# A recurrence and a max-of-two layer on one core: wd made two chunks of units at a time by strided columns, and lower_bound read by ScalarE's queue

## The chip, the cores and the metric

One NeuronCore of a Trainium2 chip, and a program of one launch. The metric is the device time of a run in microseconds (us). The kernel before took 380.85 us (median of 3 runs, 380.81 to 381.16). A ratio below is the mean time of one kernel's fast runs over that of the other's fast runs of the same rounds, so not quite the ratio of the medians that stand beside it. TensorE does the products and the transposes, VectorE, ScalarE and GpSimd the work on elements, and the sync, ScalarE and GpSimd queues issue the loads. L436 is line 436 of the kernel; in the changed kernel the lines quoted below stand five further down (L436 is L441 there). A chain of waits is read back from the last instruction: at each step to what released it, or to the instruction before it on its engine.

## The reference, cut to what matters

```python
sig = 1.0 / (1.0 + np.exp(-f_logit))                 # x, f_logit: 4 x 6144 x 256
f = lower_bound + (1.0 - lower_bound) * sig          # lower_bound: 256
h = f[:, t] * h + (1.0 - f[:, t]) * x[:, t]          # for each t; y[:, t] = h
g = np.maximum(y @ w1, y @ w2)                       # w1, w2: 256 x 1024
out = g @ w_out                                      # w_out: 1024 x 256
```

The kernel uses 1 − f = (1 − lower_bound)·(1 − sig): with om = 1 − lower_bound folded into the weights, it needs max(y w1, y w2) = y w1 + relu(y (w2 − w1)). So `wd` = om·(w2 − w1) feeds the first layer, and the part y·w1·w_out goes through `w13`, made from `w1T` and `wob` (w_out in half precision).

Of the kernel before, what the change touches and what calls it, by code (L numbers as in the profile page):

```python
# [12 lines left out]
AF = mybir.ActivationFunctionType  # L13
ENG = mybir.EngineType
P = 128
# [3 lines left out]
def kernel(  # L19
# [10 lines left out]
    nc = tc.nc  # L30
# [14 lines left out]
    for b in range(B):  # L45
        t = 0
# [49 lines left out]
    def fetch(c, s):  # L96
        b, t0, nt, _ = chunks[c]
        src = srcs[s][b, t0 : t0 + nt, :]
        if by_xbar(c, s):
            nc.gpsimd.dma_start(  # L100
                out=pieces(scratch[s][c % NSCR][:]), in_=pieces(src)
            )
        else:
            nat = inpool.tile([P, TB // P, D], HALF, name=("fT", "xT")[s])
            nc.gpsimd.dma_start(  # L105
                out=nat[:].rearrange("p i d -> p (i d)"),
                in_=src.rearrange("(p i) d -> p (i d)", p=P),
            )
            held[c, s] = nat
# [3 lines left out]
    def fetch_first(k):  # L113
        nt = TB // 2
        for s in range(2):
            raw = opool.tile([P, nt // P, D], FP32, name="osb")
            nc.sync.dma_start(  # L117
                out=raw[:],
                in_=srcs[s][0, k * nt : (k + 1) * nt, :].rearrange(
                    "(p i) d -> p i d", p=P  # L120
                ),
            )
            raws[k, s] = raw
# [37 lines left out]
    def turn_steps(j):  # L161
        b, t0, nb, c, o = blocks[j]
        steps = []
        for s in range(2):
            dst = ps_o.tile([P, KC, TB], HALF, name="ps")
            ns = nb // P
            turned[j, s] = dst[:].rearrange("p k (i m) -> p k m i", i=ns)
            for q in range(ns):
                for h in range(KC):
                    steps.append(  # L170
                        (
                            dst[:, h, q * P : (q + 1) * P],
                            held[c, s][:, q, h * P : (h + 1) * P],
                        )
                    )
        return steps
# [14 lines left out]
    def y_of(j, k):  # L191
        return rts[j, k][:, KH, :]
# [123 lines left out]
    ident_f = const.tile([P, P], FP32)  # L316
    make_identity(nc, ident_f[:])
    ident = const.tile([P, P], HALF)
    om = const.tile([P, KC], FP32)
    nom = const.tile([P, KC], FP32)  # L320
    lbc = const.tile([P, KC], FP32)
    seen = const.tile([1, 16], HALF)
    waited = const.tile([P, 1], FP32)
    warm = const.tile([P, 1], FP32)
    wob = wpool.tile([P, FC, D], HALF)
    wd = wpool.tile([P, KC, DFF], HALF)
# [6 lines left out]
    NQ = FC // NG  # L333
    w2n = [rpool.tile([P, KC, NQ * P], FP32, name="r") for g in range(NG)]
    w1n = [rpool.tile([P, KC, NQ * P], FP32, name="r") for g in range(NG)]
    w1s = [rpool.tile([P, KC, NQ * P], FP32, name="r") for g in range(NG)]
# [13 lines left out]
    def scale_w1(g):  # L350
        for kc in range(KC):
            nc.scalar.mul(w1s[g][:, kc, :], w1n[g][:, kc, :], om[:, kc : kc + 1])

    def half_w1(g, copy):
        for kc in range(KC):
            copy(out=w1h[g][:, kc, :], in_=w1s[g][:, kc, :])

    def make_wd(g):
        for kc in range(KC):
            nc.vector.scalar_tensor_tensor(  # L360
                out=wd[:, kc, g * NQ * P : (g + 1) * NQ * P],
                in0=w2n[g][:, kc, :],
                scalar=om[:, kc : kc + 1],
                in1=w1s[g][:, kc, :],
                op0=ALU.mult,
                op1=ALU.subtract,
            )

    def unit_cols(fc):

        g, q = divmod(fc, NQ)
        return slice(g * NQ * P + q, (g + 1) * NQ * P, NQ)

    def turn_w1(g):
        pt = ps_o.tile([P, NQ, KC, P], HALF, name="ps")
        for q in range(NQ):
            for kc in range(KC):
                nc.tensor.transpose(
                    pt[:, q, kc, :], w1h[g][:, kc, q : NQ * P : NQ], ident[:]
                )  # L380
        return pt

    def keep_w1T(g, pt):
        nc.vector.tensor_copy(
            out=w1T[:, g * NQ : (g + 1) * NQ, :],
            in_=pt[:].rearrange("p q k d -> p q (k d)"),
        )
# [42 lines left out]
    def first_layer(j, fc):  # L430
        k, g = divmod(fc, KH)
        if fc % 2 == 0:
            dts["d"] = ps_d.tile([P, 2, TB], FP32, name="dT")
        dT = dts["d"]
        for kc in range(KC):
            nc.tensor.matmul(  # L436
                dT[:, fc % 2, :],
                lhsT=wd[:, kc, unit_cols(fc)],
                rhs=y_of(j, kc),
                start=(kc == 0),  # L440
                stop=(kc == KC - 1),  # L441
            )
        if fc % 2:
            nc.scalar.activation(  # L444
                out=rts[j, k][:, g - 1 : g + 1, :].rearrange(
                    "p q (i m) -> p q i m", m=P
                ),
                in_=dT[:].rearrange("p q (m i) -> p q i m", m=P),
                func=AF.Relu,
            )  # L450
# [166 lines left out]
        return [runner(s) for s in steps]  # L617

    with tc.manual_schedule():
        nc.sync.dma_start(out=lbc[:], in_=lower_bound.rearrange("(h p) -> p h", p=P))  # L620
        nc.vector.tensor_copy(out=ident[:], in_=ident_f[:])
        nc.vector.tensor_scalar(
            out=om[:], in0=lbc[:], scalar1=-1.0, scalar2=1.0, op0=ALU.mult, op1=ALU.add
        )
        nc.vector.tensor_scalar_add(out=nom[:], in0=lbc[:], scalar1=-1.0)
        fetch_first(0)
        fetch_first(1)
        for g in range(NG):
# [3 lines left out]
            out=wob[:].rearrange("p (g q) c -> p g (q c)", g=NG),  # L632
            in_=moe_w_out.rearrange("(g p q) c -> p g (q c)", g=NG, q=NQ),
        )
        for c in range(1, 6):
            for s in range(2):
                fetch(c, s)
        nc.scalar.activation(out=warm[:], in_=om[:, 0:1], func=AF.Sigmoid)
        wt = ps_d.tile([P, 2, 2 * TB], HALF, name="dT")
        for q in range(8):  # L640
            nc.tensor.transpose(wt[:, 0, 0:P], ident[:], ident[:])
# [9 lines left out]
            nc.tensor.transpose(wt[:, 0, 0:P], ident[:], ident[:])  # L651
        scale_w1(0)
        half_w1(0, nc.scalar.copy)
        make_wd(0)
        pt = turn_w1(0)
        keep_w1T(0, pt)
        scale_w1(1)
        for fc in range(4):
            first_layer(0, fc)
        half_w1(1, nc.vector.tensor_copy)  # L660
        make_wd(1)
        pt = turn_w1(1)
        for fc in range(4, 8):
            first_layer(0, fc)
        keep_w1T(1, pt)
        steps = turn_steps(1)
        make_w13(0)
        turn(steps[:8])
# [118 lines left out]
```

## The kernel before: what the change touches

The work is done in blocks of 512 tokens. Block 0 has a prologue of its own, in two halves, while the weights arrive. The order of statements is the order on each engine. Cuts are marked with `# ...`.

```python
def make_wd(g):                              # one of two groups of 512 units
    for kc in range(KC):
        nc.vector.scalar_tensor_tensor(
            out=wd[:, kc, g * NQ * P : (g + 1) * NQ * P],
            in0=w2n[g][:, kc, :], scalar=om[:, kc : kc + 1], in1=w1s[g][:, kc, :],
            op0=ALU.mult, op1=ALU.subtract)

def unit_cols(fc):                           # unit chunk fc: every fourth column of its group
    g, q = divmod(fc, NQ)
    return slice(g * NQ * P + q, (g + 1) * NQ * P, NQ)
# ...
nc.sync.dma_start(out=lbc[:], in_=lower_bound.rearrange("(h p) -> p h", p=P))
nc.vector.tensor_copy(out=ident[:], in_=ident_f[:])
# om = 1 - lbc, nom = lbc - 1, both on VectorE
fetch_first(0); fetch_first(1)               # f and x of block 0, sync queue
for g in range(NG):
    fetch_w(g)                               # w1, w2 in two groups, sync queue
pool_waits(w1n[0][:, 0, 0:1])                # GpSimd waits for the first weight piece,
# ... then issues wob and f, x of blocks 1 to 3, then the scratch loads
nc.scalar.activation(out=warm[:], in_=om[:, 0:1], func=AF.Sigmoid)
# ... 8 dummy transposes
first_bf16(0, 0, nc.vector.tensor_copy)      # casts of f and x, first half of block 0
first_bf16(0, 1, nc.vector.tensor_copy)
first_turn(0)                                # transposes
first_recurrence(0)                          # sigmoid, decay, drive, scans
first_bf16(1, 0, nc.scalar.copy); first_bf16(1, 1, nc.scalar.copy)
first_turn(1); first_recurrence(1)
for q in range(24):                          # dummy transposes that keep TensorE busy
    nc.tensor.transpose(wt[:, 0, 0:P], ident[:], ident[:])
scale_w1(0)
half_w1(0, nc.scalar.copy)
make_wd(0)
pt = turn_w1(0)
keep_w1T(0, pt)                              # copy of the transposed w1, VectorE
scale_w1(1)
for fc in range(4):
    first_layer(0, fc)
half_w1(1, nc.vector.tensor_copy)            # casts, VectorE
make_wd(1)
pt = turn_w1(1)
for fc in range(4, 8):
    first_layer(0, fc)
keep_w1T(1, pt)
# ... make_w13 (needs w1T and wob), then block 1: transposes of f and x, and so on
```

## Time and profile before

| | us |
|---|---|
| median of the timed runs | 380.85 |
| the profiled execution itself | 381.55 |
| its span in the profile | 379.8 |

The lines of this profile are in the prediction below.

### The profile page before, as it was taken

Reading aid. Unit: us, or ns where it says so; the run is one execution under the profiler, and the core shown is the slowest. Engines: PE = TensorE matmul, PEld = TensorE weight load, DVE = VectorE, ACT = ScalarE, POOL = GpSimd, SP = SyncE. Lnnn points to the kernel's source line nnn. Section 1 sums busy time; section 2 is a strip of 40 time slices with the busy share of each in tenths; the row PEclk is TensorE's granted clock in tenths of the full one; section 3 lists DMA queues with packets and bytes.
Section 4 is the critical chain, followed back from the end, with each engine's and each line's share of the span. In section 5 each row is a group of like instructions: output and inputs, shape, how many; then the busy total and the mean of one; then the engine's idle time right before and its main releaser. Section 6 shows DMA issues by size and latency. Waiting matters only on the chain.

```text
span 379.8 us, 9454 instructions
## 1 busy us (share of the span) xinstructions
PE 369.1 (97%) x4076; PEld 279.9 (74%) x4076; DVE 333.0 (88%) x402; ACT 300.3 (79%) x406; POOL 37.5 (10%) x79
## 2 busy tenths in 40 slices
PE   4999999999999999999999999999999999999995
PEld 3677766777777777777777777777777777777784
DVE  4696789999999999999999999999999999999721
ACT  4846788798798888888888887987888888888740
POOL 1500103101201101102011011011011021000000
PEclk9999999999999999999999999999999999999999
DMA  7994999989999999999899999999999999970223
GB/s 249 242 226 98 265 162 256 167 156 289 195 195 276 180 190 251 202 172 285 143 257 190 219 251 278 127 263 223 182 263 212 188 268 211 192 265 3 110 113 113
DMA packets 103389, 77.17 MB, mean 203 GB/s; under 512 B 93554, under 2 KB 94066, under 8 KB 102642
## 3 DMA queue, kind: packets, MB, share of 16 engines
q1 hardware_dynamic: 100514, 51.13, 59.8%
q0 software_dynamic: 2544, 25.17, 34.5%
q8 instruction: 32, 0.52, 0.6%
q10 hardware_dynamic: 288, 0.26, 0.2%
q14 instruction: 11, 0.09, 0.1%
HBM read 53.48 MB, written 48.23 MB: 268 GB/s over the span
## 4 chain that ended last, share of the span: by engine, by line
PE 89%; DMA 4%; DVE 3%; POOL 1%; SPq 1%; ACT 0%; issue 0%
PE ps L605 42%; PE dT L436 41%; PE ps L482 6%; DMA xT<-in_x_dram 3%; DMA r<-in_moe_w_dram 1%; DVE r L230 1%; DVE S L506 1%; SPq L117 0%; PE ps L180 0%; DVE osb L496 0%; DVE v L223 0%; POOL fT L105 0%; DVE ff L213 0%; ACT r L444 0%; POOL wob L631 0%
## 5 line engine op out<-in xcount | busy, mean ns | idle before, releaser
L444 ACT ACTIVATE r<-dT 128x1024 f16<-128x1024 f32 x192 | 195.8, 1022 | 53.2 <-PE dT L436 53.0
L436 PE MATMUL dT<-r,wd 128*128 128x512 f16 x768 | 225.4, 379 | 1.0 <-DVE wd L360 0.5
L605 PEld LDWEIGHTS <-S 128*128 128x128 f16 x1680 | 110.9, 101 | 37.6 <-issue 0.6
L605 PEld LDWEIGHTS <-r 128*128 128x128 f16 x1260 | 87.3, 101 | 36.6
L230 DVE TENSOR_TENSOR_SCAN r<-ff,r,v 128x512 f16<-128x512 f16 x88 | 108.2, 1270 | 0.8
L605 PE MATMUL ps<-t,S 128*128 128x128 f16 x1260 | 97.8, 219 | 0.0
L436 PEld LDWEIGHTS <-wd 128*128 128x128 f16 x768 | 67.6, 113 | 6.4 <-DVE wd L360 1.1
L506 DVE TENSOR_TENSOR S<-r 128x2560 f16<-128x2560 f16 x42 | 62.4, 1485 | 10.1 <-ACT r L444 10.0
L605 PE MATMUL ps<-wob,r 128*128 128x128 f16 x672 | 67.4, 219 | 0.0
L506 DVE TENSOR_TENSOR S<-r,S 128x2560 f16<-128x2560 f16 x42 | 61.9, 1474 | 0.0
L285 ACT ACTIVATE u<-fT 128x512 f16<-128x512 f16 x88 | 56.0, 636 | 1.0 <-DMA fT<-scr 1.0
L213 DVE TENSOR_SCALAR ff<-u,nom 128x512 f16<-128x512 f16 (+1 forms) x98 | 31.3, 346 | 9.7 <-ACT u L207 5.3
L348 POOL CAST waited<-fT 128x1 f32<-128x1 f16 x21 | 10.8, 513 | 279.5 <-DMA fT<-scr 279.5
L605 PE MATMUL ps<-w,r 128*128 128x128 f16 x168 | 36.8, 219 | 0.0
L562 DVE TENSOR_TENSOR osb<-ps,sn 128x512 f32<-128x512 f32 x42 | 28.7, 684 | 6.8 <-ACT osb L560 5.3
L605 PE MATMUL ps<-t,r 128*128 128x128 f16 x420 | 33.4, 219 | 0.0
L605 PE MATMUL ps<-wob,S 128*128 128x128 f16 x336 | 31.4, 219 | 0.0
L223 DVE TENSOR_TENSOR v<-u,xT 128x1024 f16<-128x1024 f16 x44 | 30.1, 684 | 0.2 <-DMA xT<-scr 0.2
L482 PEld LDWEIGHTS <-r 128*128 128x128 f16 x240 | 23.9, 101 | 6.9
L482 PE MATMUL ps<-wob,r 128*128 128x256 f16 x192 | 26.8, 273 | 0.0
L550 ACT COPY sn<-ps 128x512 f32<-128x512 f32 x42 | 24.6, 587 | 1.1 <-PE ps L605 0.9
L560 ACT COPY osb<-ps 128x512 f32<-128x512 f32 x42 | 24.4, 582 | 0.5 <-PE ps L605 0.5
(56 smaller groups left out, 134.8 us busy)
## 6 DMA issues: line engine op xcount, KB each, us to landing
out_dram<-osb SPq DMA_DIRECT2D x47, 512.0 KB, 3.9
scr<-in_f_logit_dram POOLq DMA_DIRECT2D x22, 512.0 KB, 7.4
scr<-in_x_dram POOLq DMA_DIRECT2D x22, 512.0 KB, 10.4
r<-in_moe_w_dram SPq DMA_DIRECT2D x4, 512.0 KB, 6.8
fT<-in_f_logit_dram POOLq DMA_DIRECT2D x3, 256.0 KB, 9.2
xT<-in_x_dram POOLq DMA_DIRECT2D x3, 256.0 KB, 11.1
osb<-in_f_logit_dram SPq DMA_DIRECT2D x2, 256.0 KB, 4.5
osb<-in_x_dram SPq DMA_DIRECT2D x2, 256.0 KB, 4.1
```

The costliest lines, as they stand in the source:

```text
L213: nc.vector.tensor_scalar(out=ff[:, h, cols], in0=u[:, h, cols], scalar1=nom[:, h : h + 1], scalar2=1.0, op0=ALU.mult, op1=ALU.add,)
L223: nc.vector.tensor_tensor(out=like(v[:, :, cols], xT), in0=like(u[:, :, cols], xT), in1=xT, op=ALU.mult,)
L230: nc.vector.tensor_tensor_scan(out=y_of(j, h), data0=ff[:, h, o : o + TB], data1=v[:, h, o : o + TB], initial=0.0 if t0 == 0 else y_of(j - ...
L285: nc.scalar.activation(out=mids[p + NBLK, "u"][:, h, cols], in_=held[c, 0][:, h, cols], func=AF.Sigmoid, scale=-1.0,)
L436: nc.tensor.matmul(dT[:, fc % 2, :], lhsT=wd[:, kc, unit_cols(fc)], rhs=y_of(j, kc), start=(kc == 0), stop=(kc == KC - 1),)
L444: nc.scalar.activation(out=rts[j, k][:, g - 1 : g + 1, :].rearrange("p q (i m) -> p q i m", m=P), in_=dT[:].rearrange("p q (m i) -> p q i ...
L482: nc.tensor.matmul(ps[:, r, :], lhsT=left, rhs=right, start=(s == 0 and (r == 0 or j == NBLK - 1)), stop=(s == n - 1 and (r == 1 or j == N ...
L506: nc.vector.tensor_tensor(out=t[:], in0=a, in1=b, op=op)
L550: nc.scalar.copy(out=t[:], in_=bank[b][:])
L560: nc.scalar.copy(out=dst, in_=bank[b][:])
L562: nc.vector.tensor_tensor(out=dst, in0=bank[b][:], in1=snap[name][:], op=ALU.add)
L605: nc.tensor.matmul(bank[b][:, i, :], lhsT=a[:, k, cols], rhs=w, start=fresh, stop=after is not None, skip_group_check=True,)
```

## The change

Its intent is to let the first layer of block 0 begin after a quarter of wd instead of a half, to take the copies of w1T out from between, and to give the head of the sync queue to the first loads of f and x. Unit chunk fc uses every fourth column of its group, so two chunks are two neighbouring columns out of each four.

```diff
--- before.py
+++ after.py
@@ -355,13 +355,18 @@
         for kc in range(KC):
             copy(out=w1h[g][:, kc, :], in_=w1s[g][:, kc, :])
 
-    def make_wd(g):
+    def make_wd(g, pair):
+
+
+        def cut(t):
+            return t.rearrange("p (n q) -> p n q", q=NQ)[:, :, 2 * pair : 2 * pair + 2]
+
         for kc in range(KC):
             nc.vector.scalar_tensor_tensor(
-                out=wd[:, kc, g * NQ * P : (g + 1) * NQ * P],
-                in0=w2n[g][:, kc, :],
+                out=cut(wd[:, kc, g * NQ * P : (g + 1) * NQ * P]),
+                in0=cut(w2n[g][:, kc, :]),
                 scalar=om[:, kc : kc + 1],
-                in1=w1s[g][:, kc, :],
+                in1=cut(w1s[g][:, kc, :]),
                 op0=ALU.mult,
                 op1=ALU.subtract,
             )
@@ -617,12 +622,13 @@
         return [runner(s) for s in steps]
 
     with tc.manual_schedule():
-        nc.sync.dma_start(out=lbc[:], in_=lower_bound.rearrange("(h p) -> p h", p=P))
+        nc.scalar.dma_start(out=lbc[:], in_=lower_bound.rearrange("(h p) -> p h", p=P))
         nc.vector.tensor_copy(out=ident[:], in_=ident_f[:])
+        nc.scalar.activation(out=warm[:], in_=ident_f[:, 0:1], func=AF.Sigmoid)
+        nc.vector.tensor_scalar_add(out=nom[:], in0=lbc[:], scalar1=-1.0)
         nc.vector.tensor_scalar(
             out=om[:], in0=lbc[:], scalar1=-1.0, scalar2=1.0, op0=ALU.mult, op1=ALU.add
         )
-        nc.vector.tensor_scalar_add(out=nom[:], in0=lbc[:], scalar1=-1.0)
         fetch_first(0)
         fetch_first(1)
         for g in range(NG):
@@ -635,7 +641,6 @@
         for c in range(1, 6):
             for s in range(2):
                 fetch(c, s)
-        nc.scalar.activation(out=warm[:], in_=om[:, 0:1], func=AF.Sigmoid)
         wt = ps_d.tile([P, 2, 2 * TB], HALF, name="dT")
         for q in range(8):
             nc.tensor.transpose(wt[:, 0, 0:P], ident[:], ident[:])
@@ -651,18 +656,20 @@
             nc.tensor.transpose(wt[:, 0, 0:P], ident[:], ident[:])
         scale_w1(0)
         half_w1(0, nc.scalar.copy)
-        make_wd(0)
-        pt = turn_w1(0)
-        keep_w1T(0, pt)
         scale_w1(1)
-        for fc in range(4):
-            first_layer(0, fc)
+        pt0 = turn_w1(0)
+        for pair in range(2):
+            make_wd(0, pair)
+            for fc in range(2 * pair, 2 * pair + 2):
+                first_layer(0, fc)
         half_w1(1, nc.vector.tensor_copy)
-        make_wd(1)
-        pt = turn_w1(1)
-        for fc in range(4, 8):
-            first_layer(0, fc)
-        keep_w1T(1, pt)
+        pt1 = turn_w1(1)
+        for pair in range(2):
+            make_wd(1, pair)
+            for fc in range(4 + 2 * pair, 6 + 2 * pair):
+                first_layer(0, fc)
+        keep_w1T(0, pt0)
+        keep_w1T(1, pt1)
         steps = turn_steps(1)
         make_w13(0)
         turn(steps[:8])
```

## The prediction

> **What bounds the kernel now.** I read the page first, its busy shares and its forty slices.
>
> ```profile
> PE 369.1 (97%) x4076; PEld 279.9 (74%) x4076; DVE 333.0 (88%) x402; ACT 300.3 (79%) x406; POOL 37.5 (10%) x79
> ...
> PE   4999999999999999999999999999999999999995
> ```
>
> TensorE is busy in every slice but the first and the last. The next question is whether it ever waits once it is full, so I took the busy time of each engine by stretch.
>
> ```profile
> 2.00:22.50 20.50, 16.19 (x139) 12.10 (x136) 13.71 (x27) 12.47 (x21) 6.74 (x12) 1.00 1.11 278
> 22.50:30.00 7.50, 7.23 (x61) 5.19 (x62) 6.97 (x14) 4.99 (x6) 0.00 (x0) 1.00 1.00 214
> 30.00:367.00 337.00, 336.70 (x3802) 254.64 (x3800) 309.91 (x357) 280.38 (x379) 30.06 (x61) 1.00 0.97 201
> ```
>
> The columns are stretch, length, busy PE, PEld, DVE, ACT, POOL, then granted clock, DMA share, GB/s. From 30 to 367 us TensorE lacks 0.30 us in 337. No instruction of the change runs in there, so the change can only move the moment at which this block of work begins. Everything it edits lies before 20 us. The prologue is therefore what counts, and I read the chain of waits for its first 26 us.
>
> ```profile
> 0.74 0.44 SPq L620
> 1.18 0.06 issue
> 1.25 0.45 SPq L117
> ...
> 3.16 5.50 DMA r<-in_moe_w_dram
> 8.66 0.05 issue
> 8.72 0.28 POOL waited L348
> 8.99 0.81 POOL wob L631
> ...
> 11.39 11.08 DMA xT<-in_x_dram
> 22.48 0.05 issue
> 22.52 0.62 PE ps L180 x8
> 23.14 2.18 PE ps L482 x20
> ```
>
> The columns are start, length, what. The chain begins with the sync queue issuing lower_bound (L620), then x and f of block 0 and the weights. GpSimd waits for the first weight piece before it issues its own loads, and the x tile of block 2 lands at 22.48 us. That landing releases TensorE's transposes (L180). Neither the wd instructions (L360) nor the first layer (L436) of block 0 are on it. Is the DMA time in the chain latency or throughput? The DMA share of 1.11 in the first stretch above (overlapping records take it over 1) says throughput: from about 2.5 us on the transfers are limited by the engines, not by waiting.
>
> The timeline of TensorE shows how close the other path comes:
>
> ```profile
> 15.13 1.70 PE L436 MATMUL dT<-r,wd 128*128 128x512 f16 x7 [0.23 <-DVE wd L360]
> 16.67 1.04 PE L392 MATMUL ps<-wob,w1T 128*128 128x256 f16 x8
> 17.55 0.62 PE L180 MATMUL ps<-ident,fT 128*128 128x128 f16 x8
> ...
> 21.61 0.61 PE L180 MATMUL ps<-ident,fT 128*128 128x128 f16 x8
> 22.52 0.62 PE L180 MATMUL ps<-ident,xT 128*128 128x128 f16 x8 [0.30 <-DMA xT<-in_x_dram]
> ```
>
> Between the end of block 0's first layer and the landing TensorE runs without a gap, then waits only 0.30 us for x of block 2. So the compute path has 0.30 us of slack against the transfer path.
>
> **What the Trainium skill says.** "Trainium Kernel Development and Optimization", Key Constraints: transfers issued from the sync, scalar and GpSimd queues share 16 DMA engines, and several issuers save only the sequencer's issue time. The trace gives that issue time: 0.44 us for lower_bound, with the next issue at 1.25 instead of 0.74.
>
> "SBUF — State Buffer", Door 1: SBUF has 16-byte lines and wants at least two hits in a line. A pair of fp32 columns out of every four is two hits in 16 bytes, so the strided cut should not slow the reads. The kernel before has no such VectorE read, so its trace can't say.
>
> "VectorE: DVE Perf Modes", The TRN2 errata: instructions that read SBUF carry a fixed extra cost, so halving one doesn't halve its time. The trace agrees: a scan of 256 columns took 0.678 us, one of 512 took 1.272 us.
>
> "TensorE: Matmul & The Clock Gate", What's actually happening: the array starts at half rate and its start-to-start is 106.7 ns cold and 55.6 ns warm for 128 columns. The trace agrees: 24 dummy weight loads (L651) take 2.60 us, 108 ns each, and later 8 transposes go by in 0.45 us.
>
> **The change, part by part.**
>
> *lower_bound off the sync queue.* It removes one issue from the head of that queue: 1.25 − 0.74 = 0.51 us. The four loads of block 0 and the four weight pieces are issued 0.51 us earlier. Fine slices of the DMA share show about 0.2 from 1.8 to 2.3 us at 2 GB/s, which I take for the small pieces of lower_bound; the big load starts after them. The capacity regained is about 0.5 us × 0.8 = 0.4 us, with little loss as lower_bound now interleaves. As the engines are then full until the landing at 22.48, that landing moves by 0.4 to 0.5 us; I take 0.45. lower_bound itself may land a little later, since ScalarE issues it at about 0.73 and loads its table (1.28 us) after; its first use, in the decay at 5.76, has nearly 3 us of room. The warm-up activation no longer waits for om, so the table is ready by about 2.5, before the sigmoid at 5.13.
>
> *wd in pairs.* One instruction over 512 columns takes 0.744 us and the next starts about 0.65 later. At one element per 0.96 GHz cycle, 256 columns fewer save 0.27 us: an estimate of 0.48 us long, 0.38 apart. Eight of them occupy about 3.0 us instead of 2.6, so VectorE does 0.4 us more. What is won: w1T's copy leaves the way between the wd groups (0.60 us), and the second group's half-casts, wd and products move forward. On before's clock: the first pair is ready at 11.95, when the transposes of w1 free TensorE anyway; the second at 12.71; products 0 to 3 are issued by 13.64 rather than 14.05. Casts end at 13.37, the second group's transposes run to about 14.1, its pairs are ready at 14.1 and 14.9, and the last product is issued at 15.65 rather than 16.65. That is 1.0 us on TensorE.
>
> But what comes next needs other things. The product of w1T and wob (L392) needs both copies of w1T, now last on VectorE: 14.8 + 2 × 0.65 = 16.1. It needs wob as well, issued at 8.94 and 7.3 us to landing, 16.24. Then come f of block 1 (9.80 + 7.7 = 17.5) and x of block 2 at 22.48. So of the 1.0 us some 0.4 survive to the start of L392 and nothing survives the wait for x: the wait of 0.30 merely grows to about 0.7. Its worth at the end is 0.0 to 0.05 us.
>
> *Sum.* Removed from the path: 0.45 + 0.0. Added to it: nothing. 380.85 − 0.45 = 380.40 us. One later point could catch this gain: the first layer of block 4 begins at 45.61, and the second scan that it reads ends at 45.70 for a product due at 45.83, so a slack of about 0.1. That scan hangs on the scratch transfers and crossbar transposes, which come from the same GpSimd queue and the same full DMA engines, so I expect it to move along.
>
> **Rivals.**
>
> *A. The pairs pay in full.* TensorE's first layer of block 0 ends 1.0 us sooner and carries through, with 0.45 of the queue: 379.4. For it: TensorE does wait for wd (0.26 and 0.23). Against it: the chain passes through the landing at 22.48, and wob's landing at 16.24 stops it sooner.
>
> *B. Nothing moves.* The small packets of lower_bound now compete with the first big load, or the landing at 45.7 keeps its place: 380.8. For it: full DMA engines, and 0.1 us of slack there. Against it: the idle engines before 2.3 us.
>
> *C. The strided cut is slow.* Should each column cost double, eight instructions take 0.27 more each, 2.1 us; the copies of w1T end near 18.2 and L392 starts 1.1 to 1.5 us after its old place, of which 0.3 is slack: about 381.5 with the queue's gain. Against it are the line rule above and the small pieces.
>
> *D. TensorE warms later.* The clock rises near 12 us now. If it rose one product group later, 16 products would take 0.2 us more each, partly hidden: up to +2 us. The dummy transposes stay and move with the loads, so I give it little.
>
> **Range and chances.** Even A and D together stay within 0.6% of the time, while 2% is 7.6 us. The only way to over 2% is a different state of the chip or an interplay in the full region that the trace doesn't hint at. The three runs before spread over 0.35 us. I give 379.8 to 380.9 at 8 in 10: A lies below it, B inside it, C and D above it. Chances: faster 0.01, same 0.98, slower 0.01.
>
> **What would show it.** In the changed profile: the first sync issue is x or f at about 0.74; the first cast starts near 3.55 instead of 4.00; the weight landing that releases GpSimd is near 8.2; eight wd instructions of about 0.48 us; the wait of L180 for x of block 2 grows to 0.5 to 0.8 us and ends near 22.0; the stretch from 30 to 367 is as full as before. I am wrong if that wait vanishes (then compute was the bound), if x lands at 22.5 as before (the issue slot was worth nothing), if the wd instructions take 0.7 us each, or if a new wait of TensorE shows near 45 us.

## The result, and the profile after

| | before | changed |
|---|---|---|
| first four runs, median | 380.83 us | 380.98 us |
| their spread | 380.80 to 381.16 | 380.63 to 381.56 |
| the profiled execution | 381.55 | 380.66 |

The ratio is 1.0004 (0.9986 to 1.0021): within 2%, as said, but 0.08 us above my range of 379.8 to 380.9. The two profiles show 379.8 and 378.9 us of span, a gain of 0.9 that the medians don't have. The profile of before is of one of its slower runs (381.55 against a median of 380.85), the one after is of one of the faster (380.66 against 380.98). So the comparison of the two traces is no measurement of the change, and I had to separate its effect from what differs from run to run.

The lines of the changed kernel's page, and its stretch from 30 to 367 us, that answer to those of before:

```profile
PE 369.0 (97%) x4076; PEld 279.8 (74%) x4076; DVE 333.3 (88%) x406; ACT 300.4 (79%) x406; POOL 39.7 (10%) x79
...
PE   5999999999999999999999999999999999999995
```

```profile
30.00:367.00 337.00, 336.70 (x3803) 254.79 (x3801) 309.93 (x357) 280.12 (x378) 32.09 (x61) 1.00 0.96 202
```

The full region is the same to 0.01 us of TensorE's busy time (336.70 both times). That part of the prediction holds: everything happens before 30 us. Its chain of waits there (start, length, what):

```profile
0.74 0.39 SPq L117
...
2.60 5.50 DMA r<-in_moe_w_dram
8.10 0.05 issue
8.15 0.57 POOL waited L348
...
9.52 7.54 DMA fT<-in_f_logit_dram
17.06 0.05 issue
17.11 0.62 PE ps L180 x8
17.73 0.87 PE ps L397 x8
```

The weights are issued at 2.60 instead of 3.16 and land at 8.10 instead of 8.66. But the landing that releases TensorE is now f of block 1 (17.06), not x of block 2, which no longer makes anyone wait. What VectorE did, from its timeline (start, length, instruction, idle before it and what ended it):

```profile
4.46 0.17 DVE L628 TENSOR_SCALAR nom<-lbc 128x2 f32<-128x2 f32 x1 [2.89 <-DMA lbc<-in_lower_bound_dram]
...
4.60 0.42 DVE L128 CAST nat<-osb 128x512 f16<-128x512 f32 x1
...
11.06 1.65 DVE L365 SCALAR_TENSOR_TENSOR wd<-r,om 128x256 f16<-128x256 f32 x4
...
14.88 1.28 DVE L389 COPY w1T<-ps 128x1024 f16<-128x1024 f16 x2
```

Two things stand out. lower_bound lands 3.7 us after its issue instead of 2.1, and the first cast, which stands behind nom and om in VectorE's order, waits with them: it starts at 4.60, where before had 4.00 and I had 3.55. And the four wd instructions of a group take 1.65 us together, at a median of 0.479 us each and about 0.39 apart, which is the 0.48 and 0.38 that I estimated.

### The profile page after: what moved, and what is told of

The parts are those of the page before. It is cut to its first block, busy times and chain, and to the rows that moved or that the text cites. A ratio compares the mean times of both kernels' runs of the same rounds, so it can differ in the third digit from the quotient of the medians.

```text
span 378.9 us, 9458 instructions
## 1 busy us (share of the span) xinstructions
PE 369.0 (97%) x4076; PEld 279.8 (74%) x4076; DVE 333.3 (88%) x406; ACT 300.4 (79%) x406; POOL 39.7 (10%) x79
## 4 chain that ended last, share of the span: by engine, by line
PE 91%; DMA 3%; DVE 3%; SPq 0%; POOL 0%; ACT 0%; issue 0%
PE ps L610 43%; PE dT L441 41%; PE ps L487 6%; DMA fT<-in_f_logit_dram 2%; DMA r<-in_moe_w_dram 1%; DVE r L230 1%; DVE S L511 1%; PE ps L180 1%; SPq L117 0%; DVE osb L501 0%; DVE v L223 0%; DVE ff L213 0%; ACT r L449 0%; PE ps L397 0%; POOL wob L637 0%; POOL waited L348 0%
## 5 line engine op out<-in xcount | busy, mean ns | idle before, releaser
L441 PE MATMUL dT<-r,wd 128*128 128x512 f16 x768 | 225.3, 379 | 0.8 <-DVE r L230 0.3
L441 PEld LDWEIGHTS <-wd 128*128 128x128 f16 x768 | 67.6, 113 | 6.2 <-DVE wd L365 1.3
L348 POOL CAST waited<-fT 128x1 f32<-128x1 f16 x21 | 12.9, 613 | 278.0 <-DMA fT<-scr 278.0
```

Source lines behind the costliest of these rows:

```text
L441: nc.tensor.matmul(dT[:, fc % 2, :], lhsT=wd[:, kc, unit_cols(fc)], rhs=y_of(j, kc), start=(kc == 0), stop=(kc == KC - 1),)
```

## The experiments

Fifteen runs were made, all correct, each in five rounds beside the kernel before. The kernels of one call share a chip and the runs of before. "Before" beside a result is the median of those shared runs.

### The two kernels again, and the two parts alone

**e1: the kernel before, unchanged.** No edit.

> The kernel before, unchanged, run again for its spread. Its timed runs lay at 380.8 to 381.16 us while its profiled execution took 381.55 us with x of block 2 landing at 22.48 us and TensorE waiting 0.30 us for it. Theory 1 (the chain of waits of that one profile is the rule): all runs within 0.3 us of each other, and the new profile shows that landing at 22.4 to 22.6 again. Theory 2 (the time before 30 us differs from run to run, and the profile fell on a late one): runs spread over 0.5 us or more, and a profile with a time near 380.8 shows that landing at 21.6 to 22.0 and no wait of TensorE for it.

Measured: 380.82 us (380.60 to 381.86). Theory 2 held: the spread is 1.26 us, and the profile, of a run at 380.78, has no wait of TensorE for any load. Its chain of waits:

```profile
2.21 4.10 DMA osb<-in_f_logit_dram
...
10.80 1.30 DVE wd L360 x2
12.10 0.60 DVE w1T L384
12.70 0.67 DVE S L356 x2
13.37 1.34 DVE wd L360 x2
14.71 0.04 issue
14.76 1.70 PE dT L436 x7
16.46 0.87 PE ps L392 x8
```

This is a run of before at its usual time, and a different picture from the one I predicted from. From 10.80 to 14.71 VectorE is the path: wd, the copy of w1T, the casts, wd again; then the first layer of block 0 (L436). All of it is what the pairs rearrange. In this run x of block 2 was transposed at 21.67 us without a wait, against 22.52 in the first profile.

**e2: the changed kernel, unchanged.** No edit.

> The changed kernel, unchanged. Its four runs fell at 380.63, 380.66, 381.29 and 381.56 us. Theory 1: ratio to before 0.9985 to 0.9995 with a tight spread. Theory 2 (two levels in the start, in either kernel): again two levels about 0.7 us apart, ratio 0.999 to 1.001; the first cast starts at 4.4 to 4.7 us because VectorE waits for lower_bound in all of them.

Measured: 380.41 us (380.21 to 381.01), before 380.86, ratio 0.9986 (0.9971 to 1.0001). Neither theory holds as put: the ratio is theory 1's, but the spread of 0.8 us is not tight, and it is a spread rather than two levels. The wait for lower_bound is there again (the first cast at 4.61). Its chain of waits:

```profile
0.74 3.70 DMA lbc<-in_lower_bound_dram
...
8.03 2.56 PE dT L656 x24
10.59 1.04 PE ps L383 x8
11.63 2.33 PE dT L441 x8
13.96 0.45 PE ps L383 x8
14.41 1.74 PE dT L441 x8
```

With the pairs in, the path is TensorE itself. Read the same row twice: eight transposes (L383) take 1.04 us at 10.59 and 0.45 at 13.96; eight products (L441) 2.33 and then 1.74. In between TensorE's clock doubled: the trace records the moment from which the full clock was granted, here 12.59 us. So the moment of the clock's rise is now part of the time.

**e3: lower_bound alone.** The change's lines on lower_bound, the warm-up activation and nom; wd as before.

> Only the part of the change that moves lower_bound to ScalarE's queue. As I predicted it: 0.45 us faster than before (ratio 0.9988). Rival (VectorE, in order, waits for lower_bound until about 4.45 us before it may cast the first f, 0.6 us later than in the kernel before, and only the loads of the weights and of GpSimd move 0.5 us earlier): ratio 0.9995 to 1.0005, first cast at 4.4 to 4.7 us, weight landing at 8.1 us.

Measured: 381.10 us (381.06 to 381.41), before 380.86, ratio 1.0002 (0.9988 to 1.0017); the first cast at 4.63, the weights released GpSimd at 8.21. The interval alone would still allow the predicted 0.9988; the chain of waits decides for the rival:

```profile
0.74 3.72 DMA lbc<-in_lower_bound_dram
...
11.17 1.30 DVE wd L360 x2
...
13.74 1.33 DVE wd L360 x2
...
15.12 1.70 PE dT L436 x7
```

It begins at the landing of lower_bound and runs through the first cast, the transposes, the sigmoid and VectorE's scans to wd. The first wd starts 0.37 us later than in e1 and the products 0.36 (15.12 against 14.76), and the profiled run took 0.35 us more (381.13 against 380.78), though the weights do come earlier. The clock rose at about the same moment in both (12.62 and 12.50).

**e4: the pairs alone.** lower_bound on the sync queue as before.

> Only the pairs of wd, with lower_bound on the sync queue as before. As I predicted it: 0.00 to 0.05 us, ratio 0.9999 to 1.0001, the gain being eaten by the wait for x of block 2. Rival (that wait is not the rule, so the compute path is often the limit): 0.3 to 0.5 us faster, ratio 0.9987 to 0.9992.

Measured: 380.31 us (379.86 to 381.32), before 380.86, ratio 0.9981 (0.9963 to 0.9999). The rival is right, by a little more than its band: 0.55 us, and all of the change's gain (0.45 in e2).

### What holds each part's gain

**e5: casts first.** On the changed kernel:

```diff
-        (nom and om from lbc, ahead of the loads' statements)
         first_bf16(0, 0, nc.vector.tensor_copy)
         first_bf16(0, 1, nc.vector.tensor_copy)
+        (nom and om from lbc)
```

> The changed kernel with VectorE's two small instructions on lower_bound moved behind its first two casts, so that the casts no longer wait for lower_bound. Theory (the queue part of the change lost its gain to that wait, first cast at 4.6 instead of about 3.6 us): first cast at 3.4 to 3.9 us, time 0.3 to 0.6 us below the changed kernel of the job before (380.41 us), near 379.9. Rival (the first casts are not on the path, the loads of the second half of block 0 and the clock are): within 0.15 us of the changed kernel.

Measured: 380.42 us (380.01 to 380.68), before 380.82, ratio 0.9986. No better than the changed kernel of the earlier call (380.41), as the rival had it. The cast no longer waits for lower_bound, and still starts at 4.03: f itself had not landed sooner. So the wait of VectorE was not the only thing that took the gain of the issue slot. The chain of this profile goes through the landing of f of block 1 (16.98 us), which may hide what the cast won.

**e6: casts first, and TensorE kept busy early.** 24 dummy transposes instead of 8 at the start, 8 between and 7 after the first half's transposes.

> The same with more dummy transposes early: 24 instead of 8 at the start, 8 between the transposes of f and x and 7 after them, so that TensorE is busy without long gaps from 1.6 us on. Theory (in the run at 380.86 us with pairs only the array's clock rose at 13.35 us, in the others at 11.0 to 12.6 us, and products and transposes before that take twice as long and are on the path): the clock rises before 9 us in every run, 0.3 to 0.8 us below the kernel with casts first, and a spread of at most 0.5 us. Rival (the path before 12 us is VectorE's and the loads'; the clock does not matter): within 0.15 us of the kernel with casts first, the spread as wide as before.

Measured: 380.76 us (380.28 to 380.88), before 380.82, ratio 0.9995. The clock rose at 7.54 us, as wanted, and the time went up by 0.3, so the rival (an early clock doesn't pay) is nearer, though its 0.15 us was missed too; what the extra transposes cost by themselves was not separated. The profiled run's chain goes through the landing of f of block 1 again, at 17.28 us. Speeding up one path hands the end to the other.

**e7: no dummies.** The changed kernel without the 24 dummy transposes.

> The changed kernel without the 24 dummy transposes that follow block 0's own. Theory (they raise the clock in time): the clock rises after 13.5 us, the products of block 0 run at 427 ns each, and the time is 0.7 to 2 us above the changed kernel. Rival (they only stand on TensorE's path, 2.56 us of the chain of the changed kernel): 0 to 0.5 us below it.

Measured: 381.97 us (380.86 to 383.11), before 380.82, ratio 1.0028 (1.0012 to 1.0044). The theory holds: 1.55 us above the kernel with casts first of the same call, which is as fast as the changed kernel was in the call before. The profiled run is one of the faster, 381.14 us, so the slower ones have no trace. In it the clock rose at 14.20. Its chain:

```profile
11.59 3.17 PE dT L441 x8
14.76 0.45 PE ps L383 x8
15.21 1.73 PE dT L441 x8
```

Most of the first eight products of block 0 run at the low clock, 3.17 us against 1.73 for the second eight.

**e8: the copies of w1T late, nothing else.** On the kernel before:

```diff
-        pt = turn_w1(0)
-        keep_w1T(0, pt)
+        pt0 = turn_w1(0)
 # ...
-        keep_w1T(1, pt)
+        keep_w1T(0, pt0)
+        keep_w1T(1, pt1)
```

> The kernel before with one thing changed: the two copies of w1T stand behind the second group's wd; wd is made whole and lower_bound is as before. Theory (the copy of w1T between the groups, 0.60 us of the chain of the repeated run of before, is the greater part of what the pairs won): 0.3 to 0.6 us below before. Rival (the halves of wd that let the products start earlier are what counts): within 0.2 us of before.

Measured: 380.50 us (380.41 to 380.70), before 380.82, ratio 0.9992 (0.9980 to 1.0004). A difference of 0.32 in the medians fits the theory, though the interval includes no change. It would be rather more than half of what the pairs gave in e4, and a third of what they gave in e11. They were run at other times. So what the halves of wd add to it is not shown.

### Other orders of the loads, and the parts once more

**e9: lower_bound as the sync queue's third load,** behind f and x of the first half, with casts first.

> The kernel with casts first, but lower_bound issued by the sync queue as its third load, behind f and x of the first half of block 0. Theory (next to the first load on another queue, the small pieces of lower_bound take from that load what the free issue slot gave it, so that f landed at 4.03 us with the casts first and at 4.00 to 4.06 in the kernels that had lower_bound ahead of it on the sync queue): the first cast starts at 3.4 to 3.7 us and the second at 4.6 to 5.0. The time is then 0 to 0.4 us below the kernel with casts first, little because the landing of f of block 1 near 17 us stays. Rival (the landing of f is set by something else, such as the start of the transfer engines): the first cast at 4.0 us again.

Measured: 381.04 us (380.04 to 382.65), before 380.96, ratio 0.9994 (0.9976 to 1.0012). The theory on the first load holds; the line is VectorE's timeline:

```profile
3.58 0.43 DVE L128 CAST nat<-osb 128x512 f16<-128x512 f32 x1 [2.02 <-DMA osb<-in_f_logit_dram]
```

The first cast starts at 3.58, which is what I had predicted for the change itself, and the second at 4.25, earlier than expected. In the other kernels in which that cast waits for its load it starts between 4.00 and 4.28. So an empty slot at the head of the queue was worth 0.45 us to the first load against e5 (4.03), once lower_bound's small pieces were not beside it; this is one trace of this order. The time did not follow: in the profiled run, of 382.65 us, f of the second half came at 6.61, the first weight at 9.59, and the clock rose only at 15.98. Why that weight was so late is not settled.

**e10: the changed kernel a third time.** No edit.

> The changed kernel, unchanged, a third time, for the sign of the result. Its first four runs gave a ratio of 1.0004, the six of the second job 0.9986. Theory (compute path earlier by the pairs, transfers and clock varying from run to run): ratio 0.9985 to 0.9995. Rival (no gain, the second job was luck): 0.9996 to 1.0005.

Measured: 380.23 us (379.89 to 381.32), before 380.96, ratio 0.9982 (0.9967 to 0.9997), below the band that I gave for the theory. The sign is settled: over the three sets the changed kernel has a median of 380.47 us in 16 runs (379.89 to 381.56), the kernel before 380.84 in its 54 (380.54 to 382.50).

**e11: the pairs alone, again.**

> Only the pairs, again. 380.31 us against 380.86 in the first of these jobs. Theory (the pairs carry the gain, and moving lower_bound adds nothing): ratio 0.998 to 0.999, within 0.3 us of the changed kernel. Rival (both parts give a share): 0.3 us or more above the changed kernel.

Measured: 379.99 us (379.81 to 380.35), before 380.96, ratio 0.9974 (0.9959 to 0.9988): a larger gain than expected, 0.97 us, and 0.24 us below the changed kernel of the same call. Its chain:

```profile
3.17 5.09 DMA r<-in_moe_w_dram
...
11.29 2.07 PE dT L441 x8
13.36 0.45 PE ps L383 x8
13.80 1.83 PE dT L441 x8
15.64 0.90 PE ps L397 x8
```

Here the clock had risen at 9.89 us, before the products. The product of w1T and wob (L397) starts at 15.64 where e1 has 16.46; a part of these 0.82 us is the clock's, which rose at 12.50 in e1.

**e12: GpSimd's loads early.** On the changed kernel:

```diff
-        pool_waits(w1n[0][:, 0, 0:1])
+        pool_waits(raws[1, 1][:, 0, 0:1])
```

> The changed kernel with GpSimd waiting for the second half of x of block 0 instead of for the first weight piece, so that its loads are issued about 0.7 us earlier. My prediction had that wait on the path to the landing of x of block 2. Theory (the engines are full with the weights until about 11 us, so GpSimd's loads queue anyway): TensorE's transposes of f of block 1 start within 0.3 us of those of the changed kernel, time within 0.2 us. Rival (the wait is on the path): those landings 0.5 us or more earlier and the time 0.2 to 0.5 us lower.

Measured: 380.28 us (380.14 to 380.37), before 380.96, ratio 0.9979. The theory holds: 0.05 us from the changed kernel of the same call, and f of block 1 transposed at 16.63 against 16.35 there. So GpSimd's wait, a link of the chain that I had predicted from, costs nothing here. The spread of 0.23 us is the smallest of all.

**e13, e14, e15: the same on the kernel before, on the pairs alone, and on the pairs alone with early dummies.**

> The kernel before with GpSimd waiting for x of block 0 instead of for the first weight piece. Theory (the usual run of the kernel before is bound by VectorE and the first layer of block 0; the late landing adds only its slow runs): median within 0.2 us of before, no run of the late level (spread at most 0.5 us, none above 381.3). Rival (the landing is the bound, as I predicted): 0.4 us or more below before.

> Pairs only, lower_bound on the sync queue, GpSimd's loads early. Theory (two causes of spread, one of them removed): 379.8 to 380.3 us, spread at most 0.6 us, what is left following the clock. Rival (issuing early slows the weights and so the compute path): 380.3 or above.

> The same with more dummy transposes early, 24 at the start, 6 and 7 around the second transposes. Theory (with the landing early, an early clock is worth what it was in the runs at 379.8 to 379.9): the clock rises before 9 us, median 379.6 to 379.95, spread at most 0.4 us. Rival (VectorE's chain of scans and wd is the limit once the clock rises before about 10 us, and the extra transposes only delay the first ones): equal to the kernel without them, within 0.15 us, or slower.

Measured, with before at 381.00: e13 381.90 us (381.25 to 382.34, ratio 1.0013), e14 380.77 (380.64 to 384.10, 1.0005), e15 381.59 (380.69 to 382.27, 1.0006). The interval of each ratio includes no change, so none is shown to be slower than before; but the theories forecast gains or tight runs, and all three fell. The rivals of e14 and e15 (380.3 or above; no better than e14) held. VectorE's timeline of e13 shows a new wait:

```profile
14.57 1.41 DVE L360 SCALAR_TENSOR_TENSOR wd<-r,om 128x512 f16<-128x512 f32 x2 [1.05 <-DMA r<-in_moe_w_dram]
```

With lower_bound still first on the sync queue, the weights are issued 0.56 us later than in e12 (3.16 against 2.60). GpSimd's loads are now early beside them, and the last weight piece keeps wd waiting: 1.05 us in e13, 0.58 in e14, 1.18 in e15. In e15 the clock rose at 6.73 us and could not help, since TensorE waited for wd. So in these traces GpSimd's wait does useful work: it keeps the weights ahead. It was loosened without such a wait only where the weights were issued earlier (e12).

### What differs from run to run

The profiled runs of the kernels that have the pairs, sorted by time; left out are e7 without dummies and the kernels with loads in another order (e9, e12, e14, e15). The third column is the clock's rise in the trace's record, the last the end of GpSimd's own wait for f of block 1, which shows about when that load landed.

| run | time | clock rises | f of block 1 |
|---|---|---|---|
| e10, changed | 379.89 | 9.39 | 15.89 |
| e11, pairs alone | 379.99 | 9.89 | 16.16 |
| e2, changed | 380.42 | 12.59 | 16.13 |
| first profile, changed | 380.66 | 11.00 | 17.34 |
| e5, casts first | 380.68 | 9.60 | 17.26 |
| e4, pairs alone | 380.86 | 13.35 | 16.45 |
| e6, early dummies | 380.88 | 7.54 | 17.56 |

With the load early (15.9 to 16.5) the time rises with the clock's moment: 379.89 at 9.39 to 380.86 at 13.35. With the load late (17.3 to 17.6) the time is about 380.7 to 380.9 whatever the clock does. The kernel before shows both landings too: 17.78 in its first profile at 381.55 us, 16.34 in e1 at 380.78.

This rise is not all the clock's doing. The chains of e10 and e12 both run from the landing of lower_bound through VectorE to the first product; it landed at 4.12 us in e10 and at 4.40 in e12, and L397 started at 15.61 and 15.89, the same 0.28 apart, while the clock had risen before the first product in both (9.39 and 11.41). In e4 the second x of block 0 landed late, so that the 24 dummies started at 8.53 instead of 8.03 as in e2. What the clock alone is worth is read best from e7 against e12, whose chains agree up to the first product (11.59 and 11.54): with the rise at 14.20 instead of 11.41 the eight products take 3.17 us instead of 2.10, and L397 starts 1.05 us later.

Two more things stand in the traces. The full clock lasted 365.23, 368.64 or 372.05 us in each of the 17 traces, steps of 3.41 us, so the clock seems to change only at such steps, wherever they fall in an execution (inferred from these lengths). And the late landing of f of block 1 is that of GpSimd's whole queue: its first load, wob, took 7.2 to 7.4 us from issue to landing in the three late rows of the table and 5.9 to 6.2 in the four early ones.

For the clock there is an experiment, e7. For the landing there is only this table: the attempt to move it (e13 to e15) moved the weights as well. What makes that load come early or late stays open, and so does which of the two made two of the first four runs slow, since they have no trace.

## Why the prediction was wrong

**What bounds the kernel.** The step that failed first is "the x tile of block 2 lands at 22.48 us. That landing releases TensorE's transposes", taken as the bound of every run. It was true of the profiled execution, and that execution was 0.70 us slower than the median. In a run at the usual time (e1) no load makes TensorE wait after 8 us, and the path is VectorE and the first layer of block 0: rival A's picture. Right was that TensorE is full after 30 us and only the prologue counts.

**The pairs.** "Its worth at the end is 0.0 to 0.05 us": measured 0.55 and 0.97 us alone (e4, e11). What failed was the wait that I put after the gain on TensorE: in e4 and e11 TensorE waits for no load after the first product. The working of that gain had the right parts, instructions of 0.48 us and the copy leaving the way, but its 1.0 us at the last product of block 0 was the upper end. L397, which follows it, starts 0.82 us sooner in e11 than in e1, with an early clock, and 0.31 sooner in e2 (16.15), where the clock rose at nearly the same moment as in e1.

**lower_bound off the sync queue.** "I take 0.45": measured 0.24 us slower by the medians (e3, a ratio of 1.0002 that includes no change), and the changed kernel was 0.10 and 0.24 us slower than the pairs alone. Two things that I had not priced stand in the traces. With the small pieces on a queue beside it, the first load did not land sooner (4.03 with casts first, 3.58 once they are behind it). And lower_bound itself comes so late that VectorE starts the cast only at 4.60. What this second wait costs is seen in e3 against e1: 0.36 us at the first layer, on a chain that begins at that landing and has no break, so that a loss stands where I had put the gain. The chains of e2, e10 and e12 begin at the same landing. Taking the wait away did not make the kernel faster (e5), whose profile is one with the late landing of f of block 1. I wrote that "its first use, in the decay at 5.76, has nearly 3 us of room". That counted the use and not VectorE's order, where nom stands before the cast. The weights did move by 0.5 us as predicted, but in e1 and e3 the path doesn't go through them.

**The range.** The sum gave 380.40, and the pooled median of 16 runs is 380.47. That is a coincidence of two wrong terms, 0.45 for the queue and 0.0 for the pairs. The record's four runs had a median of 380.98, outside the range, because I took the spread of three timed runs, 0.35 us, for the kernel's, while its six runs in e1 spread over 1.26. Rival D, the clock, to which I gave "little", is a real term: 1.05 us at L397 between the traces of e7 and e12, and 1.55 us in the medians where the dummies are gone.

**Readings that need a correction.** The two scans that the prediction compares are not of one form: in the one form (r<-ff,r,v) 256 columns took 0.738 us and 512 took 1.272, so half the columns still took more than half the time. The spacings of 106.7 and 55.6 ns stand in the next section of the TensorE page, "Wait — 56ns, not 53.3ns?". And 7.3 and 7.7 us from issue to landing, on which the wait was built, are those of a late run: wob took 6.2 us in e1.

**Right:** the class (same), the cost of the strided cut (0.479 us measured, 0.48 estimated; the 0.27 us taken off for 256 columns is 0.744 − 0.479 = 0.265 by the traces), the unchanged full region, and no new wait near 45 us: the one wait of TensorE for a scan after 30 us is 0.3 us long in every trace.

## What to carry to other kernels

Before reading a chain of waits, compare the profiled run's own time with the median of the timed runs: a gap as large as the effect in question means that the chain may be that of another kind of run, and a second profile of the unchanged kernel is the cheapest experiment. When several paths end within a few tenths of a microsecond of each other, price a change against each of them, not only against the one that ended last. And when a load is moved to another queue, ask where its consumer stands in its engine's order and what its small pieces will travel beside.

## What the Trainium skill lacked or had wrong

- "TensorE: Matmul & The Clock Gate", Part 4: PE-mode transpose, says of transposes that the full clock "doesn't engage" for them because they don't count as busy in the same way. In e15 the clock rose at 6.73 us and in e10 at 9.39, before the first product of the program (11.26 in e10), with nothing but transposes on TensorE (the trace shows them as matmuls against the identity and doesn't say whether they carry the page's transpose mode); eight of them take 0.45 us at the full clock and 1.04 at the low one (e2).
- The same page, What's actually happening, says that the rise comes at different moments in runs of one kernel and costs under 1% of a typical span. What it lacks is that this is as large as the effect where a change of less than 1% is measured: the rise came at 9.39, 11.00 and 12.59 us in three traces of the one changed kernel, and between 11.41 (e12) and 14.20 (e7) lay 1.05 us at L397.
- "DMA: Bandwidth & Descriptors", Queues, rings and completion order, says that each engine alternates between queues packet by packet. It has no number for what a tiny load pays beside a large one: lower_bound, 1 KB, landed 2.1 us after issue ahead of the large load on its queue, and 3.4 to 3.7 us after issue beside it on another.
- No page says to check that a profiled execution is a typical one: here it was 381.55 us against a median of 380.85.
